# Linear attention and a mixture of experts: queries stream past split key sums in batches two to four

## Chip, cores, metric

One core of a Trainium2 chip runs the whole program as one launch. The metric is the device time of a launch in microseconds. The kernel before was timed three times, with a median of 959.05 us, and profiled once.

## What is computed

The first half is attention with random features; the second feeds its output, as x, to four experts whose outputs are added with weights.

```python
batch, n_heads, seq, head_dim = (4, 8, 576, 64); n_features = 128
def phi(x):                     # x scaled by 64 ** -0.25
    proj = np.einsum('bhsd,md->bhsm', x, omega)
    h = proj - np.sum(x * x, axis=-1, keepdims=True) / 2.0
    return np.exp(h - np.max(h, axis=-1, keepdims=True)) / np.sqrt(m)
kv = np.einsum('bhsm,bhsd->bhmd', k_p, v)       # k_p, q_p = phi(k_s), phi(q_s)
z = np.sum(k_p, axis=2)
num = np.einsum('bhsm,bhmd->bhsd', q_p, kv)
den = np.einsum('bhsm,bhm->bhs', q_p, z)[..., None] + 1e-06
attn_out = num / den                            # x: 2304 rows of 512
for e in range(4):                              # w1: 512 x 1024, w2: 1024 x 512
    out += p[:, e:e + 1] * (np.maximum(x @ w1[e], 0.0) @ w2[e])
```

## The kernel before

The work falls into a prologue (`begin`, L454), which makes the first half of batch one's attention, and 32 visits, numbered from 0. A visit takes half of one expert's hidden units (four tiles of 128) for a block of x rows. Four hidden steps (`hidden`, L394 to L396) make the tiles, 12 matmuls each; `relu` (L400, L401) splits each into hh and hl; then each 128 rows of the block take one output step of 12 matmuls (`outputs`, L411 to L413), which is added into acc (L418, L420). Everything is kept as a float32r value and a float32r remainder, so each product takes three matmuls. `split_w` makes that split of the weights ahead, on ACT and POOL (L377, L380), from raw tiles that SP loads.

The rest of attention is cut into ticks that are woven between these steps. `first_rest` (L584) does the second half of batch one; `later_ticks(b)` (L286) is a generator for a whole batch: batch two runs beside visits 3 to 7, three beside 8 to 15, four beside 16 to 23. A batch has four pairs of heads, 11 ticks each, and the 48 ticks of a batch are spread evenly over nine tenths of its steps (`emit`, L607). The order on each engine is the order in which this is written; nothing reorders it. All PSUM tiles come from eight banks; which bank a tile gets is settled when the program is built, and its first matmul waits until the last reader of the tile before it in that bank is done.

A pair of heads in batches two to four: `project` (L227) makes the features' exponents of keys and queries, full tiles and tails (`k_ps`, `q_ps`, `t_ps`), `exp` their exponentials kp and qp. `sum_keys` (L137) forms kv, 130 columns wide: 64 value columns and a column of ones for each of the two heads. Each full key tile is the stationary operand and 65 columns of `va` pass it; the tails of both heads share one tile, with `vb`, whose off-diagonal is zero. `turn` (L148) transposes qp on PE, and DVE copies it to qt. In `numerators` (L162) a turned query tile is stationary and the 65 columns of kv pass it, so queries lie on partitions; DVE adds epsilon to two columns, takes their reciprocal (L173) and multiplies (L175, L181) into xt. `finish` (L186) transposes xt back on PE into x_ps, and ACT and DVE split it into x_hi and x_lo (L200, L201).

```python
            p.exp("q", 1)
            p.sum_keys()
            ...
            yield
            p.turn(0, nc.vector)
            p.turn(2, nc.vector)
            yield
            p.turn(1, nc.vector)
            yield
            p.numerators(0)
            ...
            yield
            p.numerators(1)
            p.finish(0)
```

Of the kernel before, what the change touches and what calls it, by code (L numbers as in the profile page):

```python
# [6 lines left out]
F32 = mybir.dt.float32  # L7
F32R = mybir.dt.float32r
AF = mybir.ActivationFunctionType
ALU = mybir.AluOpType  # L10
# [4 lines left out]
def attention_moe(ctx, tc, kT, qT, kd, qd, kn, qn, vn, omT, probs, w1, w2, out):  # L15
# [19 lines left out]
    VW = P + 2  # L35
    WQ = 5 * P
# [22 lines left out]
    vas = [const.tile([P, 4, VW], F32, name=f"va{i}") for i in range(2)]  # L59
    vbs = [const.tile([P, NP, VW], F32, name=f"vb{i}") for i in range(2)]  # L60
# [16 lines left out]

    class Pair:
        def __init__(self, b, hp):
            self.b, self.hp = b, hp  # L80
            self.va, self.vb = vas[hp % 2], vbs[b % 2]
            self.kp = {}
            self.qx = {}
            self.num = {}
# [37 lines left out]
        def exp(self, which, g):  # L122
            ps, nm = getattr(self, f"{which}h{g}")
            n = len(GROUPS[g])
            size = "t" if n == 1 else ""
            f = att.tile([P, n, M], F32, tag=which + "p" + size, name=which + "p", bufs=2 if n == 1 else 4)
# [10 lines left out]
        def sum_keys(self):  # L137

            kv = bank("kv")[:, :VW]
            nc.tensor.matmul(kv, self.kp[2][:, 0], self.vb[:, self.hp], start=True, stop=False)  # L140
            for j in range(2):
                cs = slice(j * (D + 1), (j + 1) * (D + 1))
                for t in range(4):
                    nc.tensor.matmul(kv[:, cs], self.key_tile(j, t), self.va[:, t, cs], start=False, stop=(j == 1 and t == 3))  # L144
            self.kv = att.tile([P, VW], F32, tag="kvs", name="kvs", bufs=5)
            nc.scalar.activation(self.kv, kv, AF.Copy, scale=1.0 / M)
# [15 lines left out]
        def numerators(self, part):  # L162
            nd = bank("nd")[:, :3 * VW].rearrange("p (t c) -> p t c", t=3)
            n = 2 + part
            for t in range(2):
                for j in range(2):
                    cs = slice(j * (D + 1), (j + 1) * (D + 1))
                    nc.tensor.matmul(nd[:, t, cs], self.query_tile(j, 2 * part + t), self.kv[:, cs], start=True, stop=True)  # L168
            if part:
# [4 lines left out]
            xt = att.tile([P, 3, P], F32, tag="xt", name="xt")  # L174
            nc.vector.tensor_tensor(  # L175
                xt[:, :2].rearrange("p t (j d) -> p t j d", j=2), nd[:, :2, 1:P + 1].rearrange("p t (j d) -> p t j d", j=2),
                r[:, :2, :, None].to_broadcast([P, 2, 2, D]), ALU.mult,
            )
            for j in range(2 * part):
                own = slice(j * D, (j + 1) * D)  # L180
                nc.vector.tensor_tensor(  # L181
                    xt[:D, 2, own], nd[own, 2, 1 + j * D:1 + (j + 1) * D], r[own, 2, j:j + 1].to_broadcast([D, D]), ALU.mult
                )
# [19 lines left out]
    class Halves(Pair):  # L203
# [59 lines left out]
        def exp(self, which, j):  # L263
            ps, nb = getattr(self, which + "_ps")[j], getattr(self, "nb" + which)
            f = att.tile([P, 4, M], F32, tag=which + "p", name=which + "p", bufs=4)
# [14 lines left out]
        def key_tile(self, j, t):  # L280
            return self.kp[j][:, t]

        def query_tile(self, j, t):
            return self.qx[j][:, t]

    def later_ticks(b):  # L286
# [11 lines left out]
        for hp, p in enumerate(pairs):  # L298
# [19 lines left out]
            p.sum_keys()  # L318
# [13 lines left out]
            p.finish(0)  # L332
# [3 lines left out]
            yield  # L336
            p.finish(1)
            yield
# [16 lines left out]
    W1B, W2B, RAWB, HB, AB = 6, 6, 6, 6, 7  # L355
# [98 lines left out]
    def begin():  # L454
# [34 lines left out]
        nc.gpsimd.memset(vas[1][:, :, 0:VW:VW - 1], 1.0)  # L489
# [196 lines left out]
```

## Time and profile before

| what | us |
|---|---|
| median of three runs (958.74 to 959.5) | 959.05 |
| profiled execution | 959.87 |
| its span, first to last instruction | 958.0 |
| PE busy (5216 matmuls recorded) | 941.4 |
| DVE, ACT, POOL busy | 373.6, 342.5, 363.3 |

The span is what the page divides into shares; the execution's own time is 1.87 us longer. PE counts as busy while any matmul is under way, and a float32 matmul is recorded as two passes. The granted PE clock is full in all forty slices of the page.

### The profile page before, as it was taken

The page shows a single profiled execution, that of the slowest core. Times are in us where ns is not written, and L with a number is a line of the kernel's source. Part 1 is how long each engine was busy: PE and PEld are TensorE (multiplying, and loading weights), DVE is VectorE, ACT ScalarE, POOL GpSimd, SP SyncE. Part 2 cuts the span into 40 slices and gives each one's busy share as a digit, 9 for nine tenths or more (in the row PEclk, how much of TensorE's full clock was granted, in tenths as well). Part 3 has the DMA queues.
Part 4 walks back from the last instruction along what each step waited for, and adds up shares of the span by engine and source line. Part 5 has one row for each costly group of instructions (what it writes and reads, how often), then busy time and mean ns, then how long its engine had stood idle before and what let it go on. Part 6 is the DMA issues. An engine that isn't in the chain of part 4 may idle for free.

```text
span 958.0 us, 13688 instructions
## 1 busy us (share of the span) xinstructions
PE 941.4 (98%) x5216; PEld 798.2 (83%) x5216; DVE 373.6 (39%) x767; ACT 342.5 (36%) x806; POOL 363.3 (38%) x305
## 2 busy tenths in 40 slices
PE   7999999999999999999999999999999999999998
PEld 6888888888888888888888888888888888888887
DVE  4553464543334444443234545354211222222222
ACT  5454533442152434252335343433332321322130
POOL 2755444434232244443444443443413421431230
PEclk9999999999999999999999999999999999999999
DMA  7455424323341323323455242422402211321201
GB/s 168 119 167 173 151 79 129 123 75 102 88 138 44 127 70 123 102 76 88 129 151 155 67 140 75 138 77 89 132 23 88 88 38 51 88 73 27 88 1 66
DMA packets 60817, 94.09 MB, mean 98 GB/s; under 512 B 10192, under 2 KB 18576, under 8 KB 60752
## 3 DMA queue, kind: packets, MB, share of 16 engines
q1 hardware_dynamic: 60512, 92.92, 32.3%
q8 instruction: 41, 0.67, 0.3%
q10 hardware_dynamic: 240, 0.30, 0.1%
q14 instruction: 24, 0.20, 0.1%
HBM read 88.48 MB, written 4.72 MB: 97 GB/s over the span
## 4 chain that ended last, share of the span: by engine, by line
PE 94%; ACT 2%; DMA 1%; DVE 1%; POOL 0%; SPq 0%; issue 0%; POOLq 0%; ACTq 0%
PE g L411 14%; PE g L394 14%; PE g L413 14%; PE g L412 14%; PE g L396 14%; PE g L395 13%; PE kv L144 3%; PE nd L168 2%; PE qt_ps L153 2%; PE k_ps L236 1%; PE q_ps L236 1%; PE t_ps L240 1%; PE x_ps L190 1%; DMA k<-in_kT 1%; DMA va<-in_vn 1%; ACT hh L400 0%
## 5 line engine op out<-in xcount | busy, mean ns | idle before, releaser
L380 POOL TENSOR_TENSOR w1l<-wraw,w1h 128x512 fp32r<-128x512 f32 x124 | 159.6, 1288 | 381.8 <-ACT w1h L377 368.7
L394 PE MATMUL g<-x_hi,w1h 128*128 128x512 f32 (+1 forms) x688 | 249.1, 362 | 0.0
L396 PE MATMUL g<-x_hi,w1l 128*128 128x512 f32 (+1 forms) x688 | 244.6, 355 | 0.0
L395 PE MATMUL g<-x_lo,w1h 128*128 128x512 f32 (+1 forms) x688 | 244.1, 355 | 0.0
L401 DVE SCALAR_TENSOR_TENSOR hl<-g,hh 128x512 fp32r<-128x512 f32 (+1 forms) x172 | 104.0, 605 | 336.5 <-ACT hh L400 336.5
L411 PE MATMUL g<-w2h,hh 128*128 128x512 f32 x576 | 228.3, 396 | 0.5 <-ACT hh L400 0.5
L413 PE MATMUL g<-w2h,hl 128*128 128x512 f32 x576 | 225.0, 391 | 0.0
L412 PE MATMUL g<-w2l,hh 128*128 128x512 f32 x576 | 224.5, 390 | 0.0
L400 ACT ACTIVATE hh<-g 128x512 fp32r<-128x512 f32 (+1 forms) x172 | 91.1, 530 | 372.5 <-PE g L396 372.3
L380 POOL TENSOR_TENSOR w2l<-wraw,w2h 128x512 fp32r<-128x512 f32 x126 | 161.0, 1292 | 147.5 <-ACT w2h L377 146.9
L420 DVE SCALAR_TENSOR_TENSOR acc<-g,pr,acc 128x512 f32<-128x512 f32 x126 | 94.5, 750 | 194.3 <-PE g L413 193.9
L394 PEld LDWEIGHTS g<-x_hi,w1h 128*128 128x128 f32 x688 | 130.1, 189 | 18.4 <-issue 0.5
L396 PEld LDWEIGHTS g<-x_hi,w1l 128*128 128x128 f32 x688 | 129.9, 189 | 18.6
L395 PEld LDWEIGHTS g<-x_lo,w1h 128*128 128x128 f32 x688 | 130.1, 189 | 17.4
L413 PEld LDWEIGHTS g<-w2h,hl 128*128 128x128 f32 x576 | 108.1, 188 | 24.2 <-DVE hl L401 1.3
L411 PEld LDWEIGHTS g<-w2h,hh 128*128 128x128 f32 x576 | 108.3, 188 | 23.7 <-ACT hh L400 1.3
L412 PEld LDWEIGHTS g<-w2l,hh 128*128 128x128 f32 x576 | 108.3, 188 | 21.0
L377 ACT ACTIVATE w2h<-wraw 128x512 fp32r<-128x512 f32 x124 | 76.0, 634 | 93.3 <-issue 77.0
L377 ACT ACTIVATE w1h<-wraw 128x512 fp32r<-128x512 f32 x124 | 77.7, 627 | 0.1
L267 ACT ACTIVATE kp<-k_ps,nbk 128x128 f32<-128x128 f32 x96 | 27.4, 381 | 32.3 <-DVE nbk L261 32.3
L168 PEld LDWEIGHTS nd<-kvs,qt 128*128 128x128 f32 x256 | 32.8, 191 | 4.0 <-DVE qt L159 2.3
L168 PE MATMUL nd<-kvs,qt 128*128 128x65 f32 x256 | 32.3, 269 | 1.5 <-DVE qt L159 1.4
(84 smaller groups left out, 590.4 us busy)
## 6 DMA issues: line engine op xcount, KB each, us to landing
wraw<-in_w SPq DMA_DIRECT2D x256, 256.0 KB, 2.7
out<-acc SPq DMA_DIRECT2D x18, 256.0 KB, 2.0
va<-in_vn SPq DMA_DIRECT2D x16, 256.0 KB, 5.5
k<-in_kd SPq DMA_DIRECT2D x12, 288.0 KB, 3.0
q<-in_qd SPq DMA_DIRECT2D x12, 288.0 KB, 4.5
k<-in_kn SPq DMA_DIRECT2D x12, 288.0 KB, 4.9
q<-in_qn SPq DMA_DIRECT2D x12, 288.0 KB, 5.2
q<-in_qT SPq DMA_DIRECT2D x4, 160.0 KB, 3.4
```

What stands on the lines that cost most here:

```text
L168: nc.tensor.matmul(nd[:, t, cs], self.query_tile(j, 2 * part + t), self.kv[:, cs], start=True, stop=True)
L377: hi.activation(a, t, AF.Copy)
L380: lo.tensor_tensor(c, t, f32(a), ALU.subtract)
L394: nc.tensor.matmul(ps[:, :n], wa[:, w], x_hi[:, k, cs], start=(k == 0), stop=False)
L395: nc.tensor.matmul(ps[:, :n], wa[:, w], x_lo[:, k, cs], start=False, stop=False)
L396: nc.tensor.matmul(ps[:, :n], wc[:, w], x_hi[:, k, cs], start=False, stop=(k == KC - 1))
L400: nc.scalar.activation(ha, ps[:, :n], AF.Relu)
L401: nc.vector.scalar_tensor_tensor(hc, ps[:, :n], 0.0, f32(ha), ALU.max, ALU.subtract)
L411: nc.tensor.matmul(ps, ha[:, ts_], wa, start=(c == 0), stop=False)
L412: nc.tensor.matmul(ps, ha[:, ts_], wc, start=False, stop=False)
L413: nc.tensor.matmul(ps, hc[:, ts_], wa, start=False, stop=(c == FH - 1))
L420: nc.vector.scalar_tensor_tensor(acc[i], ps, sc, acc[i], ALU.mult, ALU.add)
```

## The change

In batches two to four, a pair's kv becomes 256 columns wide: for each head 64 value columns and 64 columns of ones, the heads in the order second, first. It is split into kv_h and kv_l, and the turned queries into qt_h and qt_l. `numerators` now holds a head's kv as the stationary operand and lets 256 (part 0) or 320 (part 1) turned queries pass it, three float32r matmuls a head, so that the result lies with features on partitions, as x needs it, and the denominator, repeated on 64 partitions, below or above it. ACT adds epsilon and moves it to the other half (dn); `divide` takes the reciprocal of all of dn and multiplies; `finish` copies into x_hi on ACT and subtracts on POOL. sum_keys and all nine transposes share one tick, split_turned, numerators, divide and finish have ticks of their own; finish(1) shares one with the next pair's project. Batch one keeps its method in the new layout of `va` and `vb`, of which there is one `vb` now; kp, qp, raw weights, hh and hl get a buffer fewer.

```diff
+    VZ = 2 * P
...
-    vas = [const.tile([P, 4, VW], F32, name=f"va{i}") for i in range(2)]
-    vbs = [const.tile([P, NP, VW], F32, name=f"vb{i}") for i in range(2)]
+    vas = [const.tile([P, 4, VZ], F32, name=f"va{i}") for i in range(2)]
+    vbs = [const.tile([P, NP, VZ], F32, name=f"vb{i}") for i in range(1)]
...
+    OWN = [slice(D + 1, 2 * D + 2), slice(0, D + 1)]
...
-            eng.dma_start(self.va[:, :, 1:P + 1], vn[self.b, :512, cols].rearrange("(t p) c -> p t c", p=P))
+            eng.dma_start(self.va[:, :, D:D + P], vn[self.b, :512, cols].rearrange("(t p) c -> p t c", p=P))
 
         def load_tails(self, eng=nc.sync):
             rows = vn[self.b, 512:].rearrange("p (h j d) -> p h j d", j=2, d=D)
-            eng.dma_start(self.vb[:D, :, 1:D + 1], rows[:, :, 0])
-            eng.dma_start(self.vb[D:, :, D + 1:P + 1], rows[:, :, 1])
+            eng.dma_start(self.vb[:D, :, P:P + D], rows[:, :, 1])
+            eng.dma_start(self.vb[D:, :, D:P], rows[:, :, 0])
...
+        def sum_keys(self):
+            kv = bank("kv")[:, :VZ]
+            nc.tensor.matmul(kv, self.kp[2][:, 0], self.vb[:, self.hp], start=True, stop=False)
+            for j in range(2):
+                cs = slice((1 - j) * P, (2 - j) * P)
+                for t in range(4):
+                    nc.tensor.matmul(kv[:, cs], self.kp[j][:, t], self.va[:, t, cs], start=False, stop=(j == 1 and t == 3))
+            self.kv_h, self.kv_l = (att.tile([P, VZ], F32R, tag=x, name=x, bufs=1) for x in ("kvh", "kvl"))
+            nc.scalar.activation(self.kv_h, kv, AF.Copy, scale=1.0 / M)
+            nc.vector.scalar_tensor_tensor(self.kv_l, kv, 1.0 / M, f32(self.kv_h), ALU.mult, ALU.subtract)
+        def turn(self):
+            main = []
+            for part in range(2):
+                ps = bank("qt_ps")
+                for j in range(2):
+                    for t in range(2):
+                        nc.tensor.transpose(ps[:, (2 * j + t) * P:(2 * j + t + 1) * P], self.qx[j][:, 2 * part + t], ident)
+                main.append(ps.rearrange("p (j t) -> p j t", j=2))
+            pt = bank("qt_ps")[:, :P]
+            nc.tensor.transpose(pt, self.qx[2][:, 0], ident)
+            whole = slice(0, 2 * P)
+            self.turned = [
+                [(main[0], whole)],
+                [(main[1], whole), (pt.rearrange("p (j t) -> p j t", j=2), slice(2 * P, 2 * P + D))],
+            ]
+            self.qt = {}
+        def split_turned(self, part):
+            n = 2 * P + part * D
+            qt_h, qt_l = (
+                att.tile([P, 2, n], F32R, tag=f"{x}1" if part else "qt", name=x, bufs=2 - part) for x in ("qth", "qtl")
+            )
+            for src, cs in self.turned[part]:
+                nc.scalar.activation(qt_h[:, :, cs], src, AF.Copy)
+                nc.vector.tensor_tensor(qt_l[:, :, cs], src, f32(qt_h[:, :, cs]), ALU.subtract)
+            self.qt[part] = qt_h, qt_l
+        def numerators(self, part):
+            n = 2 * P + part * D
+            if part:
+                ps = [bank("nd")[:, :n] for _ in range(2)]
+            else:
+                both = bank("nd")
+                ps = [both[:, j * n:(j + 1) * n] for j in range(2)]
+            dn = att.tile([P, n], F32, tag=f"dn{part}", name="dn", bufs=1)
+            qt_h, qt_l = self.qt[part]
+            for j in range(2):
+                w = slice((1 - j) * P, (2 - j) * P)
+                nc.tensor.matmul(ps[j], self.kv_h[:, w], qt_h[:, j], start=True, stop=False)
+                nc.tensor.matmul(ps[j], self.kv_l[:, w], qt_h[:, j], start=False, stop=False)
+                nc.tensor.matmul(ps[j], self.kv_h[:, w], qt_l[:, j], start=False, stop=True)
+            for j in range(2):
+                own, other = slice(j * D, (j + 1) * D), slice((1 - j) * D, (2 - j) * D)
+                nc.scalar.activation(dn[own], ps[j][other], AF.Copy, bias=EPS)
+            self.num[part] = ps, dn, n
+        def divide(self, part):
+            ps, dn, n = self.num[part]
+            nc.vector.reciprocal(dn, dn)
+            for j in range(2):
+                own = slice(j * D, (j + 1) * D)
+                nc.vector.tensor_tensor(dn[own], ps[j][own], dn[own], ALU.mult)
+        def finish(self, part):
+            _, dn, n = self.num.pop(part)
+            t0 = self.b * S + 2 * P * part
+            cut = min(n, -t0 % RING or n)
+            for a, m in ((0, cut), (cut, n - cut)):
+                if m:
+                    c = (t0 + a) % RING
+                    hi, lo = (x[:, self.hp, c:c + m] for x in (x_hi, x_lo))
+                    nc.scalar.activation(hi, dn[:, a:a + m], AF.Copy)
+                    nc.gpsimd.tensor_tensor(lo, dn[:, a:a + m], f32(hi), ALU.subtract)
...
             p.exp("q", 1)
-            p.sum_keys()
             if hp + 1 < NP:
                 pairs[hp + 1].load()
             yield
-            p.turn(0, nc.vector)
-            p.turn(2, nc.vector)
-            yield
-            p.turn(1, nc.vector)
+            p.sum_keys()
+            p.turn()
+            p.split_turned(0)
+            yield
+            p.split_turned(1)
             yield
             p.numerators(0)
             if hp + 1 < NP:
                 pairs[hp + 1].square("k")
             yield
             p.numerators(1)
-            p.finish(0)
+            p.divide(0)
             if hp + 1 < NP:
                 pairs[hp + 1].square("q")
                 pairs[hp + 1].lengths("k")
             yield
+            p.finish(0)
+            p.divide(1)
+            yield
             p.finish(1)
-            yield
+        yield
...
-    W1B, W2B, RAWB, HB, AB = 6, 6, 6, 6, 7
+    W1B, W2B, RAWB, HB, AB = 6, 6, 5, 5, 7
...
-        for t in vas[:1]:
-            nc.gpsimd.memset(t[:, :, 0:VW:VW - 1], 1.0)
-        for t in vbs[:1]:
+        def ones_a(t):
+            t = t.rearrange("p t (i d) -> p t i d", d=D)
+            nc.gpsimd.memset(t[:, :, 0], 1.0)
+            nc.gpsimd.memset(t[:, :, 3], 1.0)
+
+        def ones_b(t):
             nc.gpsimd.memset(t, 0.0)
-            nc.gpsimd.memset(t[:D, :, 0:1], 1.0)
-            nc.gpsimd.memset(t[D:, :, VW - 1:VW], 1.0)
+            nc.gpsimd.memset(t[:D, :, P + D:], 1.0)
+            nc.gpsimd.memset(t[D:, :, :D], 1.0)
+
+        ones_a(vas[0])
+        ones_b(vbs[0])
...
-        nc.gpsimd.memset(vas[1][:, :, 0:VW:VW - 1], 1.0)
+        ones_a(vas[1])
...
-        nc.gpsimd.memset(vbs[1], 0.0)
-        nc.gpsimd.memset(vbs[1][:D, :, 0:1], 1.0)
-        nc.gpsimd.memset(vbs[1][D:, :, VW - 1:VW], 1.0)
...
-        "vn": v.transpose(0, 2, 1, 3).reshape(B, S, H * D),
+        "vn": v.reshape(B, H // 2, 2, S, D)[:, :, ::-1].transpose(0, 3, 1, 2, 4).reshape(B, S, H * D),
```

The first place is on PE, between visits 4 and 5, the second pair of batch two (va, vb: values of the pair; kp, qp: exponentials). Before:

```order
L413 MATMUL g_1700<-w2h,hl 128x512
L140 MATMUL kv<-vb_80,kp 128x130
L144 MATMUL kv<-va_78,kp 128x65 x8
L153 MATMUL qt_ps<-ident,qp 128x128 x5
L394 MATMUL g_1756<-x_hi,w1h 128x512
L395 MATMUL g_1756<-x_lo,w1h 128x512
```

Now:

```order
L490 MATMUL g_1709<-w2h,hl 128x512
L284 MATMUL kv<-vb_79,kp 128x256
L288 MATMUL kv<-va_78,kp 128x128 x8
L300 MATMUL qt_ps<-ident,qp 128x128 x8
L303 MATMUL qt_ps<-ident,qp 128x128
L471 MATMUL g_1772<-x_hi,w1h 128x512
L472 MATMUL g_1772<-x_lo,w1h 128x512
```

The key sums are twice as wide, and all nine transposes follow them, where five stood before and four came a step later.

The second place is DVE in visit 5, from the residual of its third hidden step to that of the fourth and the next pair's maxima (sqk: key lengths; dn: denominators, then quotients). Before:

```order
L401 SCALAR_TENSOR_TENSOR hl<-g_1820,hh 128x512 [waits Activation_49]
L172 TENSOR_SCALAR r<-nd 128x6 [waits PE_49]
L173 RECIPROCAL r<-r 128x6 [waits DVE_49]
L175 TENSOR_TENSOR xt<-nd,r 128x256 [waits DVE_49]
L181 TENSOR_TENSOR xt<-nd,r 64x64 x2
L201 TENSOR_TENSOR x_lo<-x_ps,x_hi 128x256 [waits Activation_49]
L222 TENSOR_REDUCE sqk<-k 128x9 [waits Pool_49]
L201 TENSOR_TENSOR x_lo<-x_ps,x_hi 128x320 [waits Activation_49]
L401 SCALAR_TENSOR_TENSOR hl<-g_1872,hh 128x512 [waits Activation_49]
L247 TENSOR_REDUCE mxk<-k_ps 128x4 [waits PE_49] x2
```

Now:

```order
L478 SCALAR_TENSOR_TENSOR hl<-g_1835,hh 128x512 [waits Activation_49]
L344 RECIPROCAL dn<-dn 128x256 [waits Pool_49]
L347 TENSOR_TENSOR dn<-nd,dn 64x256 [waits DVE_49,PE_49]
L347 TENSOR_TENSOR dn<-nd,dn 64x256
L222 TENSOR_REDUCE sqk<-k 128x9 [waits Pool_49]
L344 RECIPROCAL dn<-dn 128x320 [waits Activation_49]
L347 TENSOR_TENSOR dn<-nd,dn 64x320 [waits DVE_49,PE_49]
L347 TENSOR_TENSOR dn<-nd,dn 64x320 [waits PE_49]
L478 SCALAR_TENSOR_TENSOR hl<-g_1882,hh 128x512 [waits Activation_49]
L247 TENSOR_REDUCE mxk<-k_ps 128x4 [waits PE_49] x2
L497 SCALAR_TENSOR_TENSOR acc<-g_1935,pr,acc 128x512 [waits PE_49]
```

And PE there, the end of that project and the first output step:

```order
L236 MATMUL q_ps<-om_r,q_1735 128x128 x6
L240 MATMUL t_ps<-om_r,k 64x128 [waits DVE_49,PE_49,Activation_49]
L240 MATMUL t_ps<-om_r,k 64x128 [waits DVE_49,Activation_49]
L240 MATMUL t_ps<-om_r,q_1735 64x128 x2
L488 MATMUL g_1935<-w2h,hh 128x512 [waits DVE_49,Activation_49]
L489 MATMUL g_1935<-w2l,hh 128x512 [waits Pool_49]
```

Both divisions now stand between the two residuals. The tail product of the second head takes the bank that the first multiply over 64x320 reads, and the output step the bank of the second; in visit 6 the residual stands between the divisions, and the first output step has the bank of the first multiply.

The third place is POOL in the prologue. Before:

```order
L467 MEMSET va_77 128x4x2 [waits DMAHW7_49]
L469 MEMSET vb_79 128x520
L470 MEMSET vb_79 64x4 [waits Pool_49]
L471 MEMSET vb_79 64x4
L108 TENSOR_TENSOR k<-k 64x640 [waits DMAHW6_49]
```

Now:

```order
L545 MEMSET va_77 128x4x64
L546 MEMSET va_77 128x4x64
L549 MEMSET vb_79 128x1024
L550 MEMSET vb_79 64x4x64 [waits Pool_49]
L551 MEMSET vb_79 64x4x64
L111 TENSOR_TENSOR k<-k 64x640 [waits DMAHW6_49]
```

The memset of va no longer waits for a load, and those of va and vb are larger; SP's loads into vb wait for the last of them in both kernels.

## Rows read from the trace of the kernel before

**Rows 1.** The page: busy us (share) xinstructions by engine; shares of the chain.

```profile
PE 941.4 (98%) x5216; PEld 798.2 (83%) x5216; DVE 373.6 (39%) x767; ACT 342.5 (36%) x806; POOL 363.3 (38%) x305
...
PE 94%; ACT 2%; DMA 1%; DVE 1%; POOL 0%; SPq 0%; issue 0%; POOLq 0%; ACTq 0%
```

**Rows 2.** What PE waited for, 95 to 690 us: total us, times, longest.

```profile
PE nd L168 <- DVE qt L159: 1.4, 1, 1.4
PE x_ps L190 <- DVE xt L175: 0.9, 1, 0.9
```

**Rows 3.** Timeline, PE, one pair of batch four: start, us, instructions.

```profile
511.93 0.40 PE L396 MATMUL g<-x_hi,w1l 128*128 128x512 f32 x1
...
512.39 1.90 PE L144 MATMUL kv<-va,kp 128*128 128x65 f32 x16
514.09 0.47 PE L394 MATMUL g<-x_hi,w1h 128*128 128x512 f32 x1
514.41 0.40 PE L395 MATMUL g<-x_lo,w1h 128*128 128x512 f32 x1
...
516.91 0.39 PE L411 MATMUL g<-w2h,hh 128*128 128x512 f32 x1
...
519.18 0.39 PE L412 MATMUL g<-w2l,hh 128*128 128x512 f32 x1
...
540.07 1.16 PE L236 MATMUL k_ps<-om_r,k 64*128 64x128 f32 x16
...
542.05 0.44 PE L240 MATMUL t_ps<-om_r,k 64*64 64x128 f32 x4
```

**Rows 4.** Timeline, PE: float32 over 128 columns, float32r over 256.

```profile
43.65 2.39 PE L116 MATMUL q_ps<-om,q 128*128 128x128 f32 x20
45.88 1.36 PE L153 MATMUL qt_ps<-ident,qp 128*128 128x128 f32 x5
...
235.90 0.28 PE L394 MATMUL g<-x_hi,w1h 128*128 128x256 f32 x1
...
241.18 0.28 PE L396 MATMUL g<-x_hi,w1l 128*128 128x256 f32 x1
```

**Rows 5.** Groups by form, DVE, ACT, POOL: count | busy, mean ns | idle before.

```profile
L401 DVE SCALAR_TENSOR_TENSOR hl<-g,hh 128x512 fp32r<-128x512 f32 x116 | 80.3, 692 | 266.7 <-ACT hh L400 266.7
...
L400 ACT ACTIVATE hh<-g 128x512 fp32r<-128x512 f32 x116 | 69.5, 599 | 249.7 <-PE g L396 249.6
...
L175 DVE TENSOR_TENSOR xt<-nd,r 128x256 f32<-128x256 f32 x32 | 13.6, 424 | 1.1
...
L222 DVE TENSOR_REDUCE sqk<-k 128x9 f32<-128x576 f32 x12 | 8.9, 745 | 0.0
...
L173 DVE RECIPROCAL r<-r 128x6 f32<-128x6 f32 x16 | 3.1, 192 | 0.5
...
L173 DVE RECIPROCAL r<-r 128x4 f32<-128x4 f32 x16 | 2.8, 178 | 0.5
...
L516 POOL MEMSET vb<- 128x520 f32 x1 | 0.5, 537 | 0.1
...
L68 DVE RECIPROCAL prs<-prs 128x18 f32<-128x18 f32 x1 | 0.3, 266 | 0.0
```

**Rows 6.** What the loads' queue on SP waited for.

```profile
SPq L100 <- POOL vb L471: 5.2, 1, 5.2
```

**Rows 7.** Timeline of the prologue, POOL, ACT and PE.

```profile
8.29 0.11 POOL L467 MEMSET va<- 128x8 f32 x1 [6.71 <-DMA va<-in_vn]
...
21.62 2.46 ACT L128 ACTIVATE kp<-k_ps,nm 128x128 f32<-128x128 f32 x9
...
26.57 0.39 PE L140 MATMUL kv<-vb,kp 128*128 128x130 f32 x2
```

**Rows 8.** The chain in order of time, 0 to 45 us: start, us, what.

```profile
14.72 6.38 DMA k<-in_kT
...
21.32 2.71 POOL k L108 x2
```

More of the change, by code (lines that the diff above doesn't have):

```diff
@@ L80, in __init__ @@
             self.b, self.hp = b, hp
-            self.va, self.vb = vas[hp % 2], vbs[b % 2]
+            self.va, self.vb = vas[hp % 2], vbs[0]
             self.kp = {}
@@ L125, in exp @@
             size = "t" if n == 1 else ""
-            f = att.tile([P, n, M], F32, tag=which + "p" + size, name=which + "p", bufs=2 if n == 1 else 4)
+            f = att.tile([P, n, M], F32, tag=which + "p" + size, name=which + "p", bufs=2 if n == 1 else 3)
             for i in range(n):
@@ L139, in sum_keys @@
             kv = bank("kv")[:, :VW]
-            nc.tensor.matmul(kv, self.kp[2][:, 0], self.vb[:, self.hp], start=True, stop=False)
+            cut = slice(D - 1, D - 1 + VW)
+            nc.tensor.matmul(kv, self.kp[2][:, 0], self.vb[:, self.hp, cut], start=True, stop=False)
             for j in range(2):
-                cs = slice(j * (D + 1), (j + 1) * (D + 1))
                 for t in range(4):
-                    nc.tensor.matmul(kv[:, cs], self.key_tile(j, t), self.va[:, t, cs], start=False, stop=(j == 1 and t == 3))
+                    nc.tensor.matmul(
+                        kv[:, OWN[j]], self.key_tile(j, t), self.va[:, t, cut][:, OWN[j]], start=False, stop=(j == 1 and t == 3)
+                    )
             self.kv = att.tile([P, VW], F32, tag="kvs", name="kvs", bufs=5)
@@ L166, in numerators @@
                 for j in range(2):
-                    cs = slice(j * (D + 1), (j + 1) * (D + 1))
-                    nc.tensor.matmul(nd[:, t, cs], self.query_tile(j, 2 * part + t), self.kv[:, cs], start=True, stop=True)
+                    nc.tensor.matmul(nd[:, t, OWN[j]], self.query_tile(j, 2 * part + t), self.kv[:, OWN[j]], start=True, stop=True)
             if part:
@@ L173, in numerators @@
             nc.vector.reciprocal(r, r)
[L174 to L183, printed above, removed]
+            xt = att.tile([P, 3, P], F32, tag="xt", name="xt", bufs=1)
+            for j in range(2):
+                own, src = slice(j * D, (j + 1) * D), slice(1 + (1 - j) * D, 1 + (2 - j) * D)
+                nc.vector.tensor_tensor(xt[:, :2, own], nd[:, :2, src], r[:, :2, 1 - j:2 - j].to_broadcast([P, 2, D]), ALU.mult)
+                if part:
+                    nc.vector.tensor_tensor(xt[:D, 2, own], nd[own, 2, src], r[own, 2, 1 - j:2 - j].to_broadcast([D, D]), ALU.mult)
             self.num[part] = xt
@@ L264, in exp @@
             ps, nb = getattr(self, which + "_ps")[j], getattr(self, "nb" + which)
-            f = att.tile([P, 4, M], F32, tag=which + "p", name=which + "p", bufs=4)
+            f = att.tile([P, 4, M], F32, tag=which + "p", name=which + "p", bufs=3)
             for i in range(4):
@@ L278, in exp_tails @@
                 (self.kp if which == "k" else self.qx)[2] = f
[L280 to L284, printed above, removed]
+        def sum_keys(self):
[8 more added lines that the diff above has]
+            nc.vector.scalar_tensor_tensor(self.kv_l, kv, 1.0 / M, f32(self.kv_h), ALU.mult, ALU.subtract)
@@ new lines, in split_turned @@
+        def split_turned(self, part):
+            n = 2 * P + part * D
+            qt_h, qt_l = (
+                att.tile([P, 2, n], F32R, tag=f"{x}1" if part else "qt", name=x, bufs=2 - part) for x in ("qth", "qtl")
+            )
+            for src, cs in self.turned[part]:
[4 more added lines that the diff above has]
+            n = 2 * P + part * D
+            if part:
+                ps = [bank("nd")[:, :n] for _ in range(2)]
[13 more added lines that the diff above has]
+            self.num[part] = ps, dn, n
@@ new lines, in divide @@
+        def divide(self, part):
+            ps, dn, n = self.num[part]
+            nc.vector.reciprocal(dn, dn)
+            for j in range(2):
+                own = slice(j * D, (j + 1) * D)
[10 more added lines that the diff above has]
+                    nc.gpsimd.tensor_tensor(lo, dn[:, a:a + m], f32(hi), ALU.subtract)
```

## Prediction

> **What bounds the kernel now.** I read the page's busy table and its chain first: PE is busy for 941.4 of 958.0 us, and 94% of the chain that ended last runs through it [rows 1]. A microsecond of matmul that goes is a microsecond of span, if PE does not then wait. Second, the list of what PE itself waited for in the stretch in which batches two to four are worked in (95 to 690 us): the two largest entries, 1.4 and 0.9 us, are all that matters [rows 2], so attention costs PE there its own matmuls and nothing else. Third, the timeline of one pair of batch four [rows 3], to see what a pair costs. Then prices: PE's matmuls [rows 4], the other engines' instructions [rows 5], and the prologue, where POOL and the loads lead [rows 6 to 8].
>
> **A pair on PE before.** From 511.93 to the next pair's projection at 540.07 there pass 28.14 us [rows 3], with 97 MoE matmuls of 512 columns. Ten of these take 2.27 us there (516.91 to 519.18), 0.227 each, so 97 take 21.99 and the pair's own work takes 6.15 us.
>
> **A pair on PE after.** The key sums become two float32 passes over 256 columns and sixteen over 128; nine transposes follow in the same group. A float32 pass over 128 columns takes 2.23/20 = 0.1115 us (43.65 to 45.88) [rows 4]; the old pass over 65 took (514.09 - 512.39)/16 = 0.106 [rows 3], so the doubled width is nearly free. For the 256-column pass no row exists: two cycles a column there are 512 cycles, so I take the 512-column row, 0.227; between twice 0.1115 and that it hardly matters. Sum: 25 x 0.1115 + 2 x 0.227 = 3.24, and 0.1 for leaving the float32 group, since the second MoE matmul after the key sums starts 0.32 behind the first (514.09 to 514.41), not 0.227: 3.34. The numerators become six float32r matmuls over 256 columns, 0.12 each (5.28 us for 44) [rows 4], and six over 320. For 320 I go between the 256- and the 512-column rows: 0.12 + 64 x (0.227 - 0.12)/256 = 0.147. That is 0.72 + 0.88 = 1.60. The five transposes of finish are gone. Total 4.94, so 1.21 less a pair, and **14.5 us** for twelve pairs.
>
> **Old waits that go.** The 1.4 us were numerators that stood right behind the copy of their turned queries, the 0.9 transposes behind the division [rows 2]. The second cannot occur without those transposes; the first stood where turning and numerators fell into one MoE step, and now at least one whole step of twelve matmuls, 2.72 us, lies between turn and numerators(0) in every pair. In that step ACT copies and DVE subtracts 512 columns; by 0.60 and 0.69 a piece [rows 5] the first part is split some 1.4 us after its transposes. **2.3 us**.
>
> **New waits, DVE.** Division now runs over every query and feature at once: a reciprocal on 128x256 and one on 128x320. The trace has it only on 4, 6 and 18 elements: 178, 192 and 266 ns [rows 5], a slope of 88/14 = 6.3 ns an element and 153 fixed, so 1.76 and 2.17 us. Below that, a plain operation on 256 elements takes 0.42 [rows 5]; above, I bound it at twice the slope. DVE gets about 3.3 us a pair more in all, against 39% busy [rows 1]; the average is harmless, the place matters. The order rows in the second place above show it: behind hl of the third hidden step stand reciprocal, two multiplies, lengths, reciprocal, two multiplies, and the next hl. From the end of that hidden step: hl ends at 1.35 (0.60 + 0.69), the reciprocal at 3.1, multiplies (0.42 each) at 3.95, lengths (0.745) at 4.7, the second reciprocal at 6.85, its first multiply at 7.35. PE meanwhile does six numerators (0.88), the fourth hidden step (2.72), and the projection's keys and queries (540.07 to 542.05, 2.0): 5.6 us. The tail matmul then waits for the bank that the multiply frees: 1.7 us. One visit later hl comes between the two divisions and the first output step waits for the same bank, 8.05 against 6.4: 1.65. In the other ten pairs a whole step or more lies between divide(1) and the project that needs its banks; with these durations DVE is done, in about six of them with only a microsecond to spare. The output matmuls need hl of the fourth step 11 matmuls (2.5 us) after the hidden matmuls end, and it takes 1.3, so a microsecond of lateness is free there too. **3.3 us back.** The values between ACT and DVE (dn, kv_l) make three more hops, all covered by the step between.
>
> **ACT and POOL.** ACT loses one 130-column copy and gains two splits, four dn copies and a wider copy, near 3 us a pair at 0.4 to 0.6 each; POOL gains two subtractions, under 0.8 each. What queues behind them are weight splits that are due a visit later, and relu, for which the order leaves the step as cover. If that cover is gone, the 1.0 us above is what can be lost first. One raw buffer fewer makes each weight load wait for the split before the one it waited for: four loads stay in flight, a landing takes under 3 us against some eleven for four steps. HB of 5: a hidden tile's buffer is free since the last output step of the visit before. Both I cost at nothing. kp and qp with three buffers likewise: the exps that would wait stand on ACT behind the copy of the key sums that free the buffer.
>
> **The prologue.** The ones of va now lie clear of the loaded columns, so POOL's memsets no longer wait for the load that held them until 8.29 (6.71 us) [rows 7]. They grow (0.54 us for 520 elements [rows 5], so 1.0 for 1024 and 0.3 for each of the small ones), but end near 4 us, not 9.2, and SP, which stood 5.2 us for them [rows 6], issues the tails and everything behind them earlier. The next holds are the buffers of the third pair's keys, free when the first pair is projected, about 8.5: its loads start some 2.4 us earlier, and the weights behind them. The fourth pair's keys (issued at 14.72, 6.38 us to land [rows 8]) still stand behind the first key sums, which come 0.3 to 0.5 earlier, but the queue ahead is emptier. They gate POOL's squares (21.32, 2.71 us) [rows 8] and so the third key sums at 26.57, whose exps end at 24.08 (21.62 + 2.46) [rows 7]. So 0.3 at least and 2.5 at most; I take **1.5**, between the two, as the landing time of 6.38 is long beside the others.
>
> **Sum.** -14.5 - 2.3 + 3.3 - 1.5 = -15.0, from the profiled execution's 959.87 (958.0 span) to 944.9. The median of the runs lies 0.8 lower, so I forecast **944.1 us**, 1.6% down. 0.2% (1.9 us) is about what a measurement of this kernel can tell from no change.
>
> **Rivals.** First, a dearer reciprocal. No row has it on a large tile, and three small ones fix a slope poorly. At a third above the slope, 8.4 ns, the two take 1.2 us more: two pairs lose it whole, and six lose 0.2 beyond their spare microsecond, 3.6 in all: 947.7. Chance 0.22. The Trainium skill, "VectorE: DVE Perf Modes" (under the fixed hardware budget), speaks for it: there the reciprocal iterates, with a repeat count of 8; at the page's 0.96 GHz that is an estimate of 8.3 ns an element, which the 6.3 ns of [rows 5] do not bear out.
>
> Second, PE waits for the split. The 128-column copies run on ACT in front of relu and behind weight splits that wait for the last output step; if each pair's numerators wait 0.75 us for qt_l or kv_l, 9 us of the gain go: 953. Against it: 2.72 us of PE work between turn and numerators, 1.4 needed. Chance 0.08.
>
> Third, on the other side: DVE becomes the gate. With x us of reciprocal beyond my 3.9 a pair, the two tight pairs pay x and six pay x - 1: 3.3 + 2x + 6(x - 1) exceeds the gains of 18.3 from x = 2.6, at 10.8 ns an element. At twice the slope, x = 3.6, the waits make 26: 967, slower by 8. For it: every relu residual is queued behind these reciprocals. Against: the 18-element row. Chance 0.06. The forecast itself has 0.64.
>
> **Numbers.** Low end: no new waits and the prologue's 2.5, 944.1 - 4.3 = 939.8. High end: the first rival without any gain in the prologue, 949.2, and two more for the part of the second: 951. Left out are most of the second rival and the third. Faster: 0.64 + 0.22 + 0.08 less 0.03 for worse mixes = 0.91; same 0.03; slower 0.06.
>
> **What would show it.** In the profile after: no PE instruction on x_ps in batches two to four; 72 nd matmuls 0.12 apart and 72 that are 0.147 apart; from key sums to projection 1.2 us less beside 97 MoE matmuls; reciprocals of 1.8 and 2.2 us; PE waits of under 2 us at t_ps in visit 5 and at g in visit 6, both behind DVE's dn; the third key sums near 25 us. Wrong would be: a reciprocal over 3 us, PE waits on hl, qtl or kvl in most pairs, or a pair above 5.5 us on PE.

## The result and the profile after

| | before | after |
|---|---|---|
| median, us | 959.27 (4 executions, 958.74 to 961.35) | 949.69 (4 executions, 948.01 to 950.88) |
| profiled execution, us | 959.87 | 949.36 |
| its span, us | 958.0 | 947.6 |
| mean granted PE clock, profiled execution | 1.000 | 0.998 |

The ratio is 0.9884, interval 0.9866 to 0.9903: 1.2% faster, where 1.6% was forecast (944.1 us). The time lies inside the range of 939.8 to 951.0, near its upper end.

The page after, engine times and the chain that ended last, against [rows 1]:

```profile
PE 930.1 (98%) x5084; PEld 791.7 (84%) x5084; DVE 414.5 (44%) x735; ACT 378.7 (40%) x890; POOL 383.6 (40%) x332
...
PE 93%; DVE 3%; ACT 2%; issue 1%; DMA 1%; ACTq 0%; POOL 0%; SPq 0%; DVEq 0%; POOLq 0%
```

PE still bounds the kernel, but DVE has come into the chain with 3%. What PE waited for after, 95 to 690 us (total us, times, longest), against [rows 2]:

```profile
PE g L488 <- DVE dn L347: 2.1, 1, 2.1
PE t_ps L240 <- DVE dn L347: 1.6, 1, 1.6
PE g L488 <- ACT hh L477: 1.0, 2, 0.6
```

The two old waits, on qt and xt, are gone. Two new ones stand behind DVE's division, each once, both in batch two. Of the two on hh, one of 0.5 us was there before. No wait on hl, qtl or kvl stands in the list.

Timeline of PE after, the second pair of batch four, against [rows 3] (start, us, instructions):

```profile
555.11 0.60 PE L284 MATMUL kv<-vb,kp 128*128 128x256 f32 x2
555.55 1.95 PE L288 MATMUL kv<-va,kp 128*128 128x128 f32 x16
557.33 1.04 PE L300 MATMUL qt_ps<-ident,qp 128*128 128x128 f32 x8
558.21 0.27 PE L303 MATMUL qt_ps<-ident,qp 128*128 128x128 f32 x1
...
563.77 0.28 PE L334 MATMUL nd<-qth,kvh 128*128 128x256 f32 x1
563.89 0.28 PE L335 MATMUL nd<-qth,kvl 128*128 128x256 f32 x1
...
567.20 0.30 PE L334 MATMUL nd<-qth,kvh 128*128 128x320 f32 x1
567.34 0.31 PE L335 MATMUL nd<-qth,kvl 128*128 128x320 f32 x1
...
576.35 0.83 PE L236 MATMUL k_ps<-om_r,k 64*128 64x128 f32 x10
```

A float32 pass over 256 columns takes 0.22 us (555.11 to 555.55, two), one over 128 takes 0.111, a numerator 0.12 or 0.145. From 555.11 to the next projection at 576.35 there pass 21.24 us, with 72 MoE matmuls; at 0.227 these are 16.34, and the pair's own work is 4.9 us, as forecast (4.94).

Since the MoE matmuls are the same in both kernels and a pair's projection stands behind the same one in both, the starts of the projections tell where the time went:

| projection of | before, us | after, us | difference | gained in the pair before it |
|---|---|---|---|---|
| batch two, pair 1 | 99.69 | 99.52 | -0.17 | (prologue and batch one) |
| pair 2 | 130.71 | 128.91 | -1.80 | 1.63 |
| pair 3 | 162.34 | 158.69 | -3.65 | 1.85 |
| pair 4 | 192.51 | 190.06 | -2.45 | **-1.20** |
| batch three, pair 1 | 252.30 | 250.73 | -1.57 | **-0.88** |
| pair 4 | 407.74 | 402.49 | -5.25 | 1.18, 1.24, 1.26 |
| batch four, pair 1 | 493.13 | 486.63 | -6.50 | 1.25 |
| pair 2 | 540.07 | 533.36 | -6.71 | **0.21** |
| pair 3 | 584.29 | 576.35 | -7.94 | 1.23 |
| pair 4 | 629.64 | 620.48 | -9.16 | 1.22 |
| MoE behind the last numerators | 670.93 | 660.66 | -10.27 | 1.11 |

The seven pairs of batches three and four without a new wait gain 1.21 us each on average (8.49/7). Three places fall out: two projections of batch two and the first pair of batch four. Behind 661 us only 0.1 is added.

The worst place is the projection of batch two's fourth pair. The trace after, all engines (start, us, engine, instructions, idle before and its releaser):

```profile
187.79 1.74 DVE L344 RECIPROCAL dn<-dn 128x256 f32<-128x256 f32 x1
...
190.52 0.76 DVE L222 TENSOR_REDUCE sqk<-k 128x9 f32<-128x576 f32 x1
...
191.31 0.69 DVE L478 SCALAR_TENSOR_TENSOR hl<-g,hh 128x512 fp32r<-128x512 f32 x1
191.92 2.14 DVE L344 RECIPROCAL dn<-dn 128x320 f32<-128x320 f32 x1
...
194.16 1.01 DVE L347 TENSOR_TENSOR dn<-nd,dn 64x320 f32<-64x320 f32 x2
...
194.79 0.47 PE L488 MATMUL g<-w2h,hh 128*128 128x512 f32 x1 [2.09 <-DVE dn L347]
...
195.67 0.63 PE L488 MATMUL g<-w2h,hh 128*128 128x512 f32 x1
...
196.10 0.63 PE L489 MATMUL g<-w2l,hh 128*128 128x512 f32 x1
...
196.52 0.63 PE L490 MATMUL g<-w2h,hl 128*128 128x512 f32 x1
...
198.98 0.39 PE L490 MATMUL g<-w2h,hl 128*128 128x512 f32 x1
...
199.21 0.40 PE L488 MATMUL g<-w2h,hh 128*128 128x512 f32 x1
```

PE waits 2.09 us for the division's first multiply, and then matmuls follow one another at 0.427 us (195.67, 196.10, 196.52), where 0.227 is usual and comes back at 198.98. The windows of the same stretch (us; busy by engine; PEclk, DMA share, GB/s) say the same in the granted clock:

```profile
192.00:196.00 4.00, 1.91 (x15) 1.47 (x13) 3.83 (x6) 0.79 (x2) 1.62 (x3) 0.93 0.23 66
196.00:200.00 4.00, 4.00 (x13) 3.13 (x13) 1.08 (x2) 0.20 (x1) 1.85 (x2) 0.65 0.25 65
200.00:205.00 5.00, 5.00 (x24) 4.14 (x23) 3.00 (x10) 2.70 (x9) 1.29 (x1) 1.00 0.07 10
```

For some 3 us the clock was at 1.2 instead of 2.4 GHz. Counted from the end of the MoE matmul before it, this projection and what it delays cost 6.52 us on PE beyond twelve MoE matmuls, where an undisturbed one costs 2.80: 3.7 more, 2.1 of them the wait and 1.6 the slower matmuls. The one at t_ps cost 4.77, 2.0 more, 1.6 of them the wait.

### The profile page after: what moved, and what is told of

Read it like the earlier page. It is cut to its first block, busy times and chain, and to the rows that moved or that the text cites. A ratio compares the mean times of both kernels' runs of the same rounds, so it can differ in the third digit from the quotient of the medians.

```text
span 947.6 us, 13534 instructions
## 1 busy us (share of the span) xinstructions
PE 930.1 (98%) x5084; PEld 791.7 (84%) x5084; DVE 414.5 (44%) x735; ACT 378.7 (40%) x890; POOL 383.6 (40%) x332
## 4 chain that ended last, share of the span: by engine, by line
PE 93%; DVE 3%; ACT 2%; issue 1%; DMA 1%; ACTq 0%; POOL 0%; SPq 0%; DVEq 0%; POOLq 0%
PE g L488 14%; PE g L490 14%; PE g L489 14%; PE g L471 13%; PE g L473 13%; PE g L472 13%; PE kv L288 2%; PE k_ps L236 1%; PE qt_ps L300 1%; PE q_ps L236 1%; PE k_ps L119 1%; PE t_ps L240 1%; PE nd L336 1%; PE nd L335 1%; PE nd L334 1%
## 5 line engine op out<-in xcount | busy, mean ns | idle before, releaser
L471 PE MATMUL g<-x_hi,w1h 128*128 128x512 f32 (+1 forms) x688 | 245.9, 357 | 0.0
L344 DVE RECIPROCAL dn<-dn 128x256 f32<-128x256 f32 (+1 forms) x24 | 46.6, 1943 | 0.6 <-ACT dn L339 0.6
L267 ACT ACTIVATE qp<-q_ps,nbq 128x128 f32<-128x128 f32 x96 | 27.4, 380 | 12.4 <-DVE nbq L261 12.3
```

The source lines that it names most:

```text
L471: nc.tensor.matmul(ps[:, :n], wa[:, w], x_hi[:, k, cs], start=(k == 0), stop=False)
```

## The experiments

Theory A: what is missing against the forecast is these two waits and the clock behind them. Theory B: it is elsewhere (buffers, queues on ACT and POOL, the prologue).

**Batch two's ticks spread a little tighter.**

```diff
-                span = 0.9 * 8 * sum(...)
+                span = (0.88 if b == 1 else 0.9) * 8 * sum(...)
```

> Batch two's ticks are spread over 0.88 of its steps instead of 0.9, nothing else. By the written order every pair then gets numerators(1) and divide(0) in one hidden step, finish(0) and divide(1) in the next, finish(1) and project in the one after. Theory A (the missing microseconds are PE's two long waits behind the division in batch two, 1.6 us at t_ps and 2.1 us at g, and the lower clock after the second, about 1.9 us for eight matmuls at 0.427 instead of 0.227): both waits fall under 0.5 us each, the granted clock stays at 1.00 in every slice, and the time goes from 949.7 to 944 to 945.5. Theory B (buffers, ACT's and POOL's queues and the prologue hold the rest): the time stays within 1 us of 949.7, waits turn up elsewhere, on hh, qtl or the weights.

Measured: 944.83 us, ratio 0.9835 (0.9814 to 0.9857); the profiled execution took 943.25 at a granted clock of 1.000. What PE waited for, the largest entries:

```profile
PE k_ps L119 <- ACT k L109: 4.9, 1, 4.9
PE kv L144 <- ACT kp L131: 1.6, 2, 1.3
PE x_ps L190 <- DVE xt L181: 1.1, 1, 1.1
PE g L488 <- ACT hh L477: 1.0, 2, 0.5
```

No wait on dn is left, without an instruction more or less: theory A, by one number that says how ticks fall on steps.

**The reciprocal replaced by a copy.**

```diff
-            nc.vector.reciprocal(dn, dn)
+            nc.vector.tensor_copy(dn, dn)
```

> The reciprocal in divide is replaced by a plain copy of the same tile onto itself, so the quotient is left out (the result is numerator times denominator). The order of everything stays as in the changed kernel. The copy should take 0.3 to 0.5 us where the reciprocal took 1.74 and 2.14. Theory A: PE's waits on dn go (1.6 and 2.1 us), the clock stays at 1.00, and the time comes to 943.5 to 945. Theory B: within 1 us of 949.7. If DVE also costs a little in other pairs, up to 1 us more goes (the hh wait of 0.6 in batch four is not behind a reciprocal and would stay).

Measured: 943.78 us, ratio 0.9831 (0.9808 to 0.9853); no wait on dn, the two on hh remain at 1.0 in all. So with the order unchanged, the waits are the reciprocal's. On the mean the copy was dearer than expected, in the groups of DVE (count | busy, mean ns | idle before):

```profile
L344 DVE COPY dn<-dn 128x320 f32<-128x320 f32 x12 | 10.3, 855 | 0.0
...
L344 DVE COPY dn<-dn 128x256 f32<-128x256 f32 x12 | 8.1, 671 | 0.6 <-ACT dn L339 0.6
```

These means mix unlike copies: nine of the 24 took 0.28 or 0.32 us, as expected, and the others 0.60 to 1.43.

**Fewer buffers alone, on the kernel before.**

```diff
-    W1B, W2B, RAWB, HB, AB = 6, 6, 6, 6, 7
+    W1B, W2B, RAWB, HB, AB = 6, 6, 5, 5, 7
...
-            ... name=which + "p", bufs=4)
+            ... name=which + "p", bufs=3)
```

> The kernel before with the smaller buffer counts of the change alone: kp and qp 3 instead of 4, raw weights 5 instead of 6, hh and hl 5 instead of 6. Theory A, as in the forecast: no cost, within 0.5 us of the kernel before (959.3). Theory B: the missing gain of about 4.6 us sits in the buffers, so 962 to 964; half of it would be 961.5.

Measured: 961.23 us over 12 executions, against 959.86 over 23 of the kernel before beside it, ratio 1.0010 (0.9996 to 1.0024). The means differ by 1.0 us, and the interval ends at 0.24% (2.3 us). The profiled execution shows no cost, with a span of 957.8 against 958.0 and between 95 and 690 us the same four waits as before; but of the executions none is below 959.54, and ten of the 23 before are. So theory B's 4.6 us are not here; half of it is just at the edge, and whether the buffers cost about a microsecond or nothing stays open.

**The layout alone, on the kernel before.** The diff is the part of the change on `va`, `vb`, `OWN`, `load_v`, `load_tails` and the memsets.

> The kernel before with the new layout of va and vb alone (128-column groups with ones on either side of a head's values, one vb, heads swapped, memsets clear of the loaded columns), with five raw weight buffers so that it fits; batches two to four keep their old method, two multiplies in the division where there was one. The forecast's term: 1.5 us less, 957.8. What the profile of the changed kernel shows up to 75 us: 0.2 us less, so 958.5 to 959.3. A rival: the earlier loads only change which load is late, and the gain depends on the pace of PE's first matmuls (the first q_ps group took 1.71 us there and 0.90 before); then a profile with the quick first group shows the third key sums near 24.9 and about 1 us less at 75 us.

Measured: 961.19 us over 12 executions, ratio 1.0009 (0.9996 to 1.0022). The forecast's 1.5 us of the prologue are not there; the kernel also has five raw weight buffers and a second multiply in every division, and whether these hide a gain was not tried. In its profile the third key sums start at 25.95 (26.57 before, [rows 7]), but `first_rest` starts at 43.52 against 43.65 [rows 4]. The kernel with fewer buffers and the old layout had its third key sums at 25.24, so a microsecond there is not the layout's.

**The next pair's lengths later.**

```diff
             p.project()
+            if hp:
+                p.lengths("k")
             p.maxima("k")
...
                 pairs[hp + 1].square("q")
-                pairs[hp + 1].lengths("k")
```

> The changed kernel with the next pair's lengths(k) (0.75 us on DVE) moved from between divide(0) and divide(1) to between that pair's project and its maxima. Theory A: DVE reaches divide(1) 0.75 us earlier where nothing else holds it (the wait at t_ps falls from 1.6 to about 0.85) and some 0.4 earlier where hl of the fourth hidden step stands in front (the wait at g falls from 2.1 to about 1.7); 1.2 us less, 948.5, if the clock still falls after the second wait, and 946.5 if it doesn't. Rival, that waits of this kind come from the queue behind maxima and exps: the later lengths delays bias and exps, and the time is 949.7 or more.

Measured: 947.21 us, ratio 0.9867 (0.9847 to 0.9886). The wait at t_ps is 0.9, that at g 1.6, close to what was expected (0.85 and 1.7): what stands on DVE in front of the second division sets both. Behind them the clock held.

**Each reciprocal twice.**

```diff
             nc.vector.reciprocal(dn, dn)
+            nc.vector.reciprocal(dn, dn)
```

> Each reciprocal in divide is done twice (the second undoes the first, so the quotient is left out): 3.9 us more of DVE a pair, its share of the span from 44% to 48%. The forecast's formula for a dearer reciprocal: the two tight pairs pay all 3.9, six pairs pay all but 1 us, 2 x 3.9 + 6 x 2.9 = 25 us, and more clock is lost behind the longer waits: about 975. Rival, that only places in batch two are tight and batches three and four have several us to spare: 2 to 4 pairs of batch two pay 3.9 and some clock, 958 to 966. If reciprocals do not gate PE at all: 950.

Measured: 979.83 us, ratio 1.0206 (1.0182 to 1.0230), 30 us more than the change. What PE waited for, without the entries of the prologue:

```profile
PE t_ps L240 <- DVE dn L348: 14.3, 9, 5.2
...
PE g L489 <- DVE dn L348: 4.3, 1, 4.3
PE g L491 <- DVE hl L479: 2.9, 3, 1.3
...
PE t_ps L240 <- DVE hl L479: 1.0, 1, 1.0
```

Behind DVE there are 22.5 us of waits instead of 3.7, so 18.8 more, at nine projections and not at two to four: batches three and four have a microsecond or two to spare, not several. The clock can hold the other 11: its mean was 0.984 against 0.998 in the profile of the change, and 0.014 of 979 us is 13.7, if PE works all that time.

**Key sums and turning apart.**

```diff
             p.sum_keys()
+            yield
             p.turn()
             p.split_turned(0)
-            yield
             p.split_turned(1)
             yield
```

> Key sums and turning in ticks of their own: sum_keys, then one tick later turn with both splits, so that a pair has two float32 groups between float32r matmuls where the change has one; the number of ticks stays. Forecast's price of one entry into float32 work and back: 0.1 us, so 1.2 us for twelve pairs (951 from 949.7) as long as the numerators behind find their operands; the split of the second part now comes in the same tick as that of the first, a tick before its numerators as before. Rival: grouping is free on PE and the time stays at 949.7; or the wait on qtl, which the change does not show, comes back with 0.3 us or more in several pairs: 953 to 954.

Measured: 950.82 us, ratio 0.9911 (0.9894 to 0.9928), against 949.69 and, in a second measurement, 949.54 of the change; the intervals overlap. On PE key sums cost 2.28 and turning 1.03 us beside the MoE matmuls, together 3.31 where the joint group costs 3.22: the 0.1 of the forecast. Waits on qth and qtl stand in its profile, which the change does not have (0.7 and 0.2 us, once each).

**Both: batch two at 0.88 and the lengths late.**

> Batch two spread over 0.88 of its steps, with the lengths(k) moved as well. With 0.88 alone no wait on dn is left on PE, so theory A expects no more than 0.3 us beyond it: 944.5. If DVE was still late in places that show as waits on hl or as a lower clock, it gains up to 1.5: 943.3. Rival, the later lengths delays maxima, bias and exps in all pairs: 945.5 to 947.

Measured: 943.98 us, ratio 0.9836 (0.9815 to 0.9857): no different from 0.88 alone.

**Batch four spread as well.**

```diff
-                span = (0.88 if b == 1 else 0.9) * 8 * sum(...)
+                span = {1: 0.88, 2: 0.9, 3: 0.83}[b] * 8 * sum(...)
```

The reason is the third place that fell out of the table of projections. Before, the key sums shared a tick with `exp("q", 1)`, and in batch four's first pair their 1.8 us of PE time lay between the third and the fourth hidden step, while ACT worked off the exponentials. The change put them a tick later, behind the first output step. Timeline of PE there, in the profile of the change:

```profile
510.19 0.39 PE L490 MATMUL g<-w2h,hl 128*128 128x512 f32 x1
511.05 0.50 PE L488 MATMUL g<-w2h,hh 128*128 128x512 f32 x1 [0.47 <-ACT hh L477]
511.38 0.40 PE L489 MATMUL g<-w2l,hh 128*128 128x512 f32 x1
511.77 0.50 PE L490 MATMUL g<-w2h,hl 128*128 128x512 f32 x1
512.11 0.59 PE L284 MATMUL kv<-vb,kp 128*128 128x256 f32 x2
```

Four matmuls take 1.92 us instead of 0.91. On ACT four exponentials of `q_ps` (from 509.34 on, 1.17 us) stood in front of the fourth hidden tile's relu, which began at 510.34, 2 us after its matmuls.

> Batch two spread over 0.88, lengths(k) late, and batch four spread over 0.83 of its steps instead of 0.9, so that no step of exponentials of query tiles or tails stands in front of the fourth hidden tile's relu without key sums behind it. Two PE waits on hh are left in the version with 0.88 and late lengths alone, 0.5 and 0.55 us, and about 1.0 us is lost around the first (1.92 us for four matmuls from 510.19 to 512.11 in the changed kernel, 0.91 at full pitch). Theory: both go, 1.5 to 2 us, from 944.0 to 942.3. Rival: the exponentials are late in any place and the wait moves to kv or the numerators: 943.5 to 944.5.

Measured: 942.71 us, ratio 0.9806 (0.9784 to 0.9828); PE waits on hh no more. The interval overlaps that of the version before it (0.9815 to 0.9857), so the waits show this gain, and the times alone do not.

**Batch one spread as well.**

```diff
-                n, per = 0, 14 / 11.0
+                n, per = 0, 14 / 11.5
```

> As the version with batch four paced, and batch one's ticks per step 14/11.5 instead of 14/11, so that numerators(1) and finish(1) of its third pair no longer stand in one step. There PE waits 1.1 us for the division (x_ps on xt, near 74 us), and in three of the profiles so far the next matmuls run at 0.21 instead of 0.12 (256 columns) for some 3 to 4 us. Theory: the 1.1 us go and the pace stays, together 1.1 in a run in which the clock held and about 2.8 in one in which it fell: 940 to 941.5. Rival: another of batch one's steps waits in its place: 942 to 942.5.

Measured: 939.92 us, ratio 0.9775 (0.9759 to 0.9791), executions from 939.45 to 940.04. All that PE waited for in the whole profile:

```profile
PE k_ps L119 <- ACT k L109: 4.9, 1, 4.9
PE kv L144 <- ACT kp L131: 1.6, 2, 1.3
PE nd L172 <- DVE qt L164: 0.2, 1, 0.2
PE x_ps L190 <- DVE xt L181: 0.2, 1, 0.2
```

**The change once more**, beside the last two:

> The changed kernel itself once more, beside the two others on one chip. Expected: 948 to 951, with 1.0 to 1.2% gain over the kernel before. If it is one of the runs in which the clock also holds behind the long wait at g (as it did behind the wait of 1.6 us at that place with the late lengths), 947.

Measured: 949.54 us, ratio 0.9885 (0.9864 to 0.9906). Its profile has the same two waits, 1.6 and 2.1 us. But the clock held behind them, and fell after batch one's wait of 1.1 us. Windows of this second profile:

```profile
74.00:78.00 4.00, 3.81 (x20) 3.58 (x21) 1.17 (x4) 2.46 (x8) 0.00 (x0) 0.67 0.30 105
78.00:82.00 4.00, 4.00 (x34) 4.00 (x34) 1.45 (x5) 1.61 (x5) 2.57 (x2) 0.91 0.17 66
...
192.00:196.00 4.00, 2.02 (x34) 1.66 (x32) 3.83 (x5) 0.90 (x3) 1.95 (x2) 1.00 0.25 87
196.00:200.00 4.00, 3.89 (x17) 3.25 (x18) 2.60 (x5) 1.00 (x2) 2.13 (x2) 1.00 0.03 13
```

So the lower clock is not tied to the new waits: the same wait of 2.1 us was followed by it in the first profile of the change and not in this one.

## Why the prediction was right, and where it was off

| step | forecast, us | profile, us |
|---|---|---|
| a pair on PE, twelve times | -14.5 | -14.5 (12 x 1.21, read from seven pairs) |
| old waits gone | -2.3 | -2.3 (none of [rows 2] left) |
| new waits behind the division | +3.3 | +5.7 (3.7 waits, 1.6 clock, 0.4 around the first) |
| ACT, POOL, buffers | 0 | +1.0 (hh, batch four) |
| prologue | -1.5 | -0.2 |
| sum | -15.0 | -10.3 |

The two profiled executions differ by 10.5, the medians by 9.6: about two thirds of the 15 forecast. The 5.7 is what batch two is short of, if its four pairs gained 1.21 each and the 2.3 of the old waits.

**The pair** came out as priced, part by part: the float32 group at 3.22 (3.34 forecast), the numerators at 0.71 and 0.88 (0.72 and 0.88), finish at nothing.

**The division.** The groups of DVE after, by form, beside [rows 5]:

```profile
L344 DVE RECIPROCAL dn<-dn 128x320 f32<-128x320 f32 x12 | 25.7, 2142 | 0.0
L344 DVE RECIPROCAL dn<-dn 128x256 f32<-128x256 f32 x12 | 20.9, 1744 | 0.6 <-ACT dn L339 0.6
...
L347 DVE TENSOR_TENSOR dn<-nd,dn 64x320 f32<-64x320 f32 x24 | 11.7, 489 | 1.3
L347 DVE TENSOR_TENSOR dn<-nd,dn 64x256 f32<-64x256 f32 x24 | 10.1, 422 | 1.0
```

Forecast were 1.76 and 2.17 us; (2142 - 1744)/64 is 6.2 ns an element, against 6.3 from the small tiles. The first rival, at 8.4, falls. The estimate of 8.3 ns from the repeat count of 8 and the clock in the Trainium skill, "VectorE: DVE Perf Modes" (under the fixed hardware budget), is not borne out by this trace. The waits stood where they were placed, at t_ps in visit 5 and at g in visit 6, 1.6 and 2.1 against 1.7 and 1.65, and went with the reciprocal and with the spreading.

**What the sum failed to hold** is the time after a wait. The step counted a wait as PE's idle time alone; in this profile the matmuls behind the second also cost 1.6 us at 1.2 GHz. That is the larger part of the term's error in this profile. The lower clock is partly chance: in the second profile of the change it held here and fell near 75 us, and the spans are 947.6 and 947.3.

**ACT at nothing** was wrong at one place. The text named the condition (relu has a step as cover, and 1.0 us is what can be lost first), and 1.0 was lost. It looked for new work in front of relu; what mattered was the key sums that moved away and had been its cover. Fewer buffers, put at nothing too, cost between nothing and 2.3 us on the kernel before; the undisturbed pairs after, at 1.21, leave them no room.

**The prologue's 1.5** failed as a step: "They gate POOL's squares and so the third key sums" was followed to the third key sums (25.72 after, 25 forecast) and no further. Of their 0.85 us 0.5 is left at 43.16 and 0.2 at the first projection. The layout alone gained nothing measurable. The traces show where the lead goes: the first MoE matmul still starts 0.85 us earlier (35.30 against 36.15), and then PE waits for DVE, 0.25 us for xt (ready at 37.00, where the matmul before leaves room at 36.80) and 0.16 for qt (ready at 37.59):

```profile
37.05 0.44 PE L190 MATMUL x_ps<-ident,xt 128*128 128x128 f32 x2
37.65 1.10 PE L172 MATMUL nd<-kvs,qt 128*128 128x65 f32 x8 [0.16 <-DVE qt L164]
```

Before, the matmuls follow one another there. DVE reached this division (its first instruction on `r`) at 36.12 against 36.65, only 0.53 us earlier. The followed path was PE's and POOL's, and DVE's was left out. One pair of profiles is weak evidence here: the third key sums start anywhere from 24.19 to 25.95 in the eleven profiles with the new layout, at 25.24 and 26.57 in the two with the old. In those in which the clock held until then, `first_rest` starts at 42.55 to 43.52 (six) and at 43.04 and 43.65 (two), 0.35 us earlier on the mean.

**The rivals.** PE waiting for splits: no wait in the change. DVE as the gate: the condition was not met, since the reciprocal cost what the small tiles said. Its arithmetic comes out at three quarters: 3.9 us more of reciprocal a pair made 18.8 us more of waits, where the formula gives 25 (2 x 3.9 + 6 x 2.9), and the clock came on top.

## What to carry to other kernels

When work moves from the engine that bounds the kernel to one with time to spare, look for its price where ticks crowd: here it was paid in two projections of twelve. List such places and shift the ticks, before the operation is made cheaper. Three numbers that set how ticks fall on steps, with one reduction moved, gave 9.6 us here (949.54 to 939.92, on one chip); the change itself gave 9.6 in its first measurement and 12.4 in its second (medians). Batch one's number is not tied to the change; what spreading gives the kernel before was not tried. And when an instruction moves, ask what it used to cover where it stood.

## What was not expected of the hardware

- In ten profiles batch one's wait of 1.13 us (x_ps on xt, near 74 us) is there. In four of them the clock fell behind it, in six it held. Where it fell, 256-column matmuls took 0.21 us each instead of 0.12 for 3 to 4 us. In the version without that wait it held, in the one profile there is; three of its four executions had a mean clock of 1.000, and none of the nine of the change over 0.998.
- The clock also fell behind a wait that the kernel before has too, that of the fourth key sums on kp (1.3 us), in five of the thirteen profiles: those of the copy, the two reciprocals, the turning apart, the late lengths and batch four's spreading. From these key sums to `first_rest` 12.2 to 13.8 us passed in the five, and 11.4 to 11.7 in the six with the same layout in which the clock held, so a fall here costs 0.5 to 2.4 us. That is as much as some of the effects that the runs above are about: look at the granted clock of both profiles before their spans are compared. In the profile with the late lengths PE waits up to 30.04, the granted clock is 0.50 from 32 to 36 us and 0.65 from 36 to 40, and 256-column matmuls start 0.21 us apart:

```profile
30.04 0.49 PE L144 MATMUL kv<-vb,kp 128*128 128x130 f32 x2 [1.28 <-ACT kp L131]
...
36.40 0.41 PE L472 MATMUL g<-x_hi,w1h 128*128 128x256 f32 x1
36.61 0.41 PE L473 MATMUL g<-x_lo,w1h 128*128 128x256 f32 x1
```

- In all thirteen profiles, each time that the clock fell while PE still had work, PE had just waited (1.13 us in the shortest case); what decides between falling and holding, no run here shows. The Trainium skill, "TensorE: Matmul & The Clock Gate" (Part 1), has the clock follow how busy PE has lately been: that it fell only behind waits agrees with it.
- PE's first matmuls differ between executions too: the eight passes of the first `q_ps` took 0.90 us in the profile before (8.53 to 9.43) and 1.71 in that of the change (8.89 to 10.60), with a granted clock of 1.00 in both rows. A comparison of two single profiles in the first 30 us is no better than that.
- The same copy of a float32 tile onto itself on DVE took 0.28 to 1.40 us for 256 elements on 128 partitions, and 0.32 to 1.43 for 320. All fifteen that took 0.60 us or more ran beside operations on POOL; of the nine short ones five did too, so that POOL is the cause is not shown. The reciprocals in the same place had no such spread: 1.74 us and 2.14, each within 0.01.
